# Three reorderings of DMA issues in a fused gated-recurrence and maxout kernel: the first gate tile in two halves, two weight pieces ahead of unit 3's k and q, and a late placing of w1 times w_out

## The chip, the cores and the metric

The kernel runs on one core of one Trainium2 chip. The metric is device time in microseconds, from the first to the last instruction and what lies around it; lower is better. A core has five engines that run their own instruction streams and wait for each other by semaphores: TensorE (PE in the profile, with PEld for its weight loads), VectorE (DVE), ScalarE (ACT), GpSimd (POOL) and SyncE (SP). SP computes nothing; here it issues nearly all DMAs, and an instruction that only issues a DMA stands in the profile under SPq or ACTq.

## The reference

```python
q, k, v, f_logit: (4, 8, 768, 48) float32          # batch, heads, time, head dimension
f = 1 / (1 + exp(-f_logit))
for t in range(768):
    state = f[:, :, t, :, None] * state + einsum('bhd,bhe->bhde', k[:, :, t], v[:, :, t])
    y[:, :, t] = einsum('bhd,bhde->bhe', q[:, :, t], state)
x = y.transpose(0, 2, 1, 3).reshape(3072, 384)
out = maximum(maximum(x @ w1, x @ w2), x @ w3) @ w_out   # w1, w2, w3: 384 x 768; w_out: 768 x 384
```

The weights w1, w2, w3 and w_out arrive as 64-bit floats and are rounded to float32 on the chip.

## The kernel before, in words

**Units.** The recurrence is cut in chunks of 64 time steps. A unit is one chunk of two batches, so there are 24 units (NU), and four of them (GRP) make a group of 512 tokens that goes through the feed-forward part together. For each unit the program calls, among others:

- `load(u)`, which loads f, k and q, and `load_v(u)`. Units 0 to 5 (u < BY_ROWS) are loaded by rows of time, one DMA of 192 KB for each of f, k and q (line 174). From unit 6 on, one call with an even u loads f, k or q of two units in eight smaller DMAs (line 183). v takes two DMAs per unit (line 164).
- `sigmoids(u)`: the gate. For the first six units PE transposes f (L291) and ACT takes the sigmoid of it (L308); later ACT works on the loaded blocks (L311).
- `scan(u)`: for later units DVE turns the gate (L296, tile `gate`), then runs a scan (L329, tile `r`).
- `after(u)` and `before(u)`: the decayed keys kh (L340) and queries qh (L351). For later units DVE turns k and q (L296, tiles `kt` and `qt`), there is a second scan between them (L347, tile `prod`), and POOL does the multiplications.
- `keys_by_blocks`: DVE turns kh back (L382, tile `ks`). `pairs`, `values`, `sums`, `finish`: the matmuls of the recurrence. `pack`: two DMAs that fill gaps in `xT`, the transposed x of a group (L524).

**Weights.** There are 24 pieces of 384 KB. `load_weights(count)` issues the next `count` of them on SP (L218); the first three go to tiles `raw`, the next nine to `placed`. A piece is then rounded by ACT (L240, L241, L244), DVE (for the first three pieces L251 and L252) and POOL (L258), and w1's piece is subtracted from those of w2 and w3 (L752).

**The feed-forward part.** `ffn_first` handles group 0 while it rounds the weights, with plain matmuls (L542). It also computes w1 times w_out (`linear`, L783) into `w_nat`, which is a part of the tile `w_in[0]`. Its function `place(dst, src, n)` copies 48-row strips of a weight within on-chip memory to the head-by-head layout of later groups, in ten DMAs for one weight (L458, L465). `placed[1]` receives w3 less w1; `w_lin`, another part of `w_in[0]`, receives `w_nat`. `ffn(g)` handles groups 1 to 5 (PE L881 for the inputs, L629 for the outputs) with fewer products, for which POOL and DVE form sums (`hm`, L899, L924, L931, L932, L593). For group 1 alone, the function `fourth(0)` calls `mix_x`, POOL's first reader of `w_lin` (L585); PE reads `w_lin` after that.

**Order.** The whole program stands in a manual schedule: each engine runs its instructions in the order in which the Python code emits them. The feed-forward part is cut into steps by Python generators; `fill(ns)` emits steps until an estimated budget of TensorE time is used, and so mixes them with the units. SP's order is also the order of the code. The main loop runs over u from 4 to 23; what it emits at u belongs mostly to unit u + 1. In it, `load(u + 2, one, "q")` at u = 8 loads q of units 10 and 11. Each new DMA takes one of eight semaphores in turn and first waits for the DMA that used it eight DMAs earlier.

**The start.** The order of the first issues is written out by hand, on SP but for three of them on ACT:

```python
load(0, both)                      # f, q on SP; k on ACT
load(1, (nc.scalar, nc.sync))      # f, q on ACT; k on SP
load_v(0)
load(2, one, "f")
load_v(1)
load(2, one, "kq")
load(3)
load_weights(3)
load_v(2)
load_v(3)
load_weights(6)
```

Of the kernel before, what the change touches and what calls it, by code (L numbers as in the profile page):

```python
# [9 lines left out]
FP32 = mybir.dt.float32  # L10
# [36 lines left out]
C = 64  # L47
# [8 lines left out]
def kernel(  # L56
# [13 lines left out]
    B, H, S, D = q.shape  # L70
# [4 lines left out]
    NK = DM // 128  # L75
    DFF = moe_w1.shape[1]
    NJ = DFF // 128
    GRP = 4
# [6 lines left out]
    w_in = [const.tile([128, NK, DFF], FP32, name=f"w_in{i}") for i in range(3)]  # L85
    w_out = const.tile([128, NJ, DM], FP32, name="w_out")
    w_nat, w_lin = w_in[0][:, :, 0:DM], w_in[0][:, :, DM:2 * DM]
    low = const.tile([1, 1], I32, name="low")

    def fast():  # L90
        ctx = ExitStack()
        with ctx:
# [48 lines left out]
            NAMES = "fkq"  # L141
# [25 lines left out]
            def load(u, queues=one, names="fkq"):  # L167
                for nm, src in (("f", f_logit), ("k", k), ("q", q)):
                    if nm not in names:
                        continue  # L170
                    if u < BY_ROWS:

                        c, bp = divmod(u, 2)
                        queues[NAMES.index(nm) % 2].dma_start(  # L174
                            out=rows[nm][u % 4][:, :, 0:D],
                            in_=src[2 * bp:2 * bp + 2, :, c * C:(c + 1) * C, :].rearrange("b h t d -> t b h d"))
                    elif u % 2 == 0:
                        t0 = u // 2 * C
                        for n in range(C // 32):
                            for par in range(2):  # L180
                                for e0, w in ((0, 32), (32, D - 32)):
                                    p0 = par * DP + e0
                                    nc.sync.dma_start(
                                        out=blocks[nm][u // 2 % 2][p0:p0 + 32, n, :, 0:w],
                                        in_=src[:, par::2, t0 + n * 32:t0 + (n + 1) * 32, e0:e0 + w].rearrange(
                                            "b h t d -> t (b h) d"))

            def load_v(u, queues=one):
                load_tokens(v_tiles[u % NLD], v, u, queues)
# [603 lines left out]
            def ffn_first(xT):  # L793
                hm = new_hm()
                steps = [(j, slice(n * HALF, (n + 1) * HALF)) for n in range(2) for j in range(J_HALF)]
                steps += [(j, slice(0, TOK)) for j in range(J_HALF, NJ)]
                n_step = 0
                for j, t in steps:
                    w = t.stop - t.start
                    for i in (1, 2):  # L800
                        p = yield from product(xT, j, i, t)
                        if i == 1:
                            nc.scalar.copy(hm[:, j, t], p)
                        else:
                            nc.vector.scalar_tensor_tensor(hm[:, j, t], hm[:, j, t], 0.0, p, op0=ALU.max, op1=ALU.max)
                        round_to(ROUNDED[n_step])
                        load_weights(2, rounded[0] - 1)
                        yield (1 if w == TOK else NK) * w * COLUMN
                        n_step += 1
                        if n_step in TURNED:  # L810
                            yield from turn(TURNED[n_step])
                for n in range(2 * NK + 2):
                    place(placed[0].bitcast(FP32), w_in[1], n)
                for a in range(NK):
                    for n, cost in enumerate(linear(a)):
                        round_to(rounded[0] + 1)
                        if a == 0 and n:
                            mix(n - 1)
                        if a == 0 and n == NK - 1:
                            mix(n)  # L820
                        yield cost
                for dst, src in ((placed[1].bitcast(FP32), w_in[2]), (w_lin, w_nat)):
                    for n in range(2 * NK + 2):
                        place(dst, src, n)
                mix(3)
                made = [[lambda jj=jj: sums_of_hm(hm, jj, slice(0, 2))] for jj in range(HJ)]
                made[-1] += [lambda jj=jj: sums_of_hm(hm, jj, slice(2, 3)) for jj in range(HJ)]
                made += [[], [], [], [], [], []]
                made += [[lambda jj=jj: sums_of_hm(hm, jj, slice(3, 4)) for jj in range(HJ)]]
                made += [[lambda: mix(4)]] + [[lambda n=n: mix_in(n)] for n in range(2)]  # L830
                made = iter(made)
                for cost in outputs_by_pairs(0, hm, xT):
                    for make in next(made, ()):
                        make()
                    yield cost
# [162 lines left out]
            with tc.manual_schedule():  # L998
# [3 lines left out]
                load(2, one, "f")  # L1002
                load_v(1)
                load(2, one, "kq")
                load(3)
                load_weights(3)
                load_v(2)
                load_v(3)
                load_weights(6)
                xT = x_tiles[0]  # L1010
                sigmoids(0)
                scan(0)
# [64 lines left out]
                for u in range(GRP, NU):  # L1077
                    n = u + 1
                    part = EARLY if u < BY_ROWS else LATER if u < 2 * GRP else PART
                    if n == BY_ROWS:  # L1080
                        scan(n)
                    fill(part)
                    keys_by_blocks(u, 2)
                    room_of_unit = room_of_pairs()
                    if u > GRP:
                        values(u - 1)
                        sums(u - 1, room_of_unit)
                    keys(u)
                    pairs(u, room_of_unit)
                    if u > GRP:  # L1090
                        finish(u - 1, xT)
                        if u % GRP == 3:
                            pack(0, 2, xT)
                        elif u % GRP == 0:
                            pack(3, 3, xT)
                    if u % GRP == 0:
                        if u > GRP:
                            packed[u // GRP - 1] = xT
                            pending.append(ffn(u // GRP - 1, xT))
                        xT = x_tiles[u // GRP % 2]  # L1100

                    if u + 2 <= BY_ROWS:
                        load(u + 2)
                    if u == BY_ROWS:
                        load(u + 2, one, "f")
                    elif u + 1 != BY_ROWS and BY_ROWS <= u + 3 < NU and u % 2:
                        load(u + 3, one, "fkq" if u % GRP == 1 else "f")
                    if u + 2 < NU:
                        load_v(u + 2)
                    keys_by_blocks(u, 3)  # L1110
                    if n < NU:
                        if n < BY_ROWS or n == BY_ROWS + 2:
                            sigmoids(n)
                        if n != BY_ROWS:
                            scan(n)
                    fill(part)
                    if n < NU:
                        after(n)
                        before(n)
                    if u == 2 * GRP:  # L1120
                        mix_in(2, nc.vector)
                    check_range(u - CHECKS, 0)
                    fill(part)
                    if BY_ROWS < u + 2 < NU and u % GRP == 0:
                        load(u + 2, one, "k")
                    if u == BY_ROWS:
                        load(u + 2, one, "kq")
                    if n < NU:
                        carry(n)
                    else:  # L1130
                        values(u)
                    check_range(u - CHECKS, 1)
                    fill(part)
                    if BY_ROWS < u + 2 < NU and u % GRP == 0:
                        load(u + 2, one, "q")
                    if n == NU:
                        finish(u, xT)
                        pack(3, 3, xT, both)
                        packed[u // GRP] = xT
                    keys_by_blocks(n, 0)  # L1140
                    fill(part - 1000 if u < 2 * GRP else part)
                    keys_by_blocks(n, 1)
                    check_range(u - CHECKS, 2)
                    if u + 2 >= CHECKS:
                        check_load(u + 2 - CHECKS)
                    if BY_ROWS <= u + 2 < NU and u != BY_ROWS:
                        sigmoids(u + 2)
# [269 lines left out]
```

## Time and profile before

| | |
|---|---|
| time of three runs | 408.34 us median, 408.01 to 408.77 |
| profiled execution, its own time | 408.11 us |
| span of the profiled execution | 406.4 us (the other 1.7 us lie around it) |
| PE busy | 390.6 us, 96% |
| DVE busy | 298.4 us, 73% |
| POOL busy | 256.4 us, 63% |
| ACT busy | 181.1 us, 45% |
| DMA: HBM read, written | 37.75 MB, 4.72 MB; mean 104 GB/s |
| granted TensorE clock | 1.000 |

The share of busy time is a mean over very different stages. By 40 slices of about 10 us, PE is below nine tenths only in the first four; DVE is at nine tenths in many slices up to about 325 us and then falls off. Over the first 60 us the DMA engines are busy most of the time.

### The profile page before, as it was taken

What the parts mean: (1) busy time and instruction counts of PE and PEld (TensorE: products, weight loads), DVE (VectorE), ACT (ScalarE), POOL (GpSimd) and SP (SyncE); (2) the same over time, 40 slices, a digit from 0 to 9 for tenths busy, and PEclk for the clock granted to TensorE, in tenths of its full rate; (3) what the DMA queues carried; (4) which work ended last, traced back from release to release, by engine and by line L of the source; (5) the groups of instructions that cost most, each with busy time, mean ns of one, the idle gap of its engine ahead of it and who ended that gap; (6) DMA issues with size and microseconds to landing.
All of it is one profiled execution on the core that took longest, in us unless ns stands there. A gap on an engine that the chain in (4) does not pass through costs nothing.

```text
span 406.4 us, 11673 instructions
## 1 busy us (share of the span) xinstructions
PE 390.6 (96%) x4658; PEld 339.5 (84%) x4658; DVE 298.4 (73%) x572; ACT 181.1 (45%) x431; POOL 256.4 (63%) x283
## 2 busy tenths in 40 slices
PE   4988999999999999999999999999999999999994
PEld 4766765559998888998889988899988899988994
DVE  6997797999988999897998997998995450012500
ACT  2479787422224441435442344523354335576210
POOL 2179695779997797397586277667477850525710
PEclk9999999999999999999999999999999999999999
DMA  8988996767367576476645376634573003541002
GB/s 173 241 260 251 275 244 88 156 93 147 92 96 115 74 156 134 84 120 85 125 109 99 57 116 88 150 83 81 77 158 86 1 19 102 131 152 47 2 19 63
DMA packets 181594, 47.21 MB, mean 116 GB/s; under 512 B 160480, under 2 KB 179232, under 8 KB 181536
## 3 DMA queue, kind: packets, MB, share of 16 engines
q1 hardware_dynamic: 178048, 45.62, 54.7%
q10 hardware_dynamic: 3488, 0.81, 1.0%
q8 instruction: 37, 0.61, 0.7%
q14 instruction: 21, 0.17, 0.1%
HBM read 37.75 MB, written 4.72 MB: 104 GB/s over the span
## 4 chain that ended last, share of the span: by engine, by line
PE 83%; DVE 6%; SPq 3%; POOL 3%; DMA 2%; issue 1%; ACT 1%; POOLq 0%
PE p L629 18%; PE p L881 17%; PE tr L881 15%; PE tr L629 13%; PE p L542 7%; PE y L415 3%; PE p L783 3%; PE a L396 2%; PE y L504 2%; PE a L433 2%; SPq L174 2%; DMA raw<-in_moe_w_dram 2%; DVE ks L382 1%; POOL w_in L258 1%; SPq L164 1%
## 5 line engine op out<-in xcount | busy, mean ns | idle before, releaser
L382 DVE STREAM_TRANSPOSE ks<-kh 32x128 f32<-32x128 f32 x256 | 77.4, 302 | 11.1 <-POOL kh L340 6.9
L881 PE MATMUL tr<-xT,placed 128*128 128x256 f32 x180 | 44.4, 384 | 0.0
L339 POOL COPY ends<-r 128x8 f32<-128x8 f32 x24 | 8.6, 357 | 48.7 <-DVE r L329 48.7
L881 PEld LDWEIGHTS tr<-xT,placed 128*128 128x128 f32 x180 | 33.6, 190 | 4.8
L329 DVE TENSOR_TENSOR_SCAN r<-gate,from_one 128x520 f32<-128x520 f32 x24 | 33.2, 1382 | 6.0 <-ACT gate L308 2.8
L340 POOL TENSOR_TENSOR kh<-kt,r 128x512 f32<-128x512 f32 x18 | 31.9, 1772 | 8.5 <-DVE kt L296 8.5
L542 PE MATMUL p<-xT,w_in 128*128 128x256 f32 (+1 forms) x108 | 33.9, 458 | 3.3 <-POOL w_in L752 2.2
L593 POOL TENSOR_TENSOR w_in<-hm 128x256 f32<-128x256 f32 x18 | 13.3, 739 | 32.2 <-DVE hm L932 29.5
L511 ACT COPY xT<-y 64x256 f32<-64x256 f32 (+1 forms) x60 | 22.1, 368 | 22.0 <-PE y L504 21.3
L347 DVE TENSOR_TENSOR_SCAN prod<-gate,from_inv 128x520 f32<-128x520 f32 x24 | 31.6, 1317 | 0.0
L881 PE MATMUL tr<-xT,w_in 128*128 128x256 f32 x120 | 30.8, 379 | 0.0
L881 PE MATMUL p<-w_in,placed 128*128 128x256 f32 x120 | 30.4, 382 | 0.0
L637 DVE TENSOR_TENSOR o<-tr,w_in 128x384 f32<-128x384 f32 (+1 forms) x11 | 5.7, 521 | 33.4 <-PE tr L629 29.0
L542 PEld LDWEIGHTS p<-xT,w_in 128*128 128x128 f32 x108 | 19.5, 190 | 12.3 <-issue 6.0
L629 PE MATMUL p<-placed,hm 128*128 128x192 f32 x144 | 29.7, 333 | 0.0
L881 PE MATMUL p<-xT,placed 128*128 128x256 f32 x120 | 29.2, 379 | 0.0
L629 PE MATMUL tr<-w_out,w_in 128*128 128x192 f32 x144 | 28.6, 326 | 0.0
L924 DVE TENSOR_TENSOR hm<-tr,hm 128x512 f32<-128x512 f32 x15 | 10.3, 684 | 22.8 <-PE tr L881 15.9
L258 POOL TENSOR_TENSOR w_in<-top_bits,rest_bits 128x384 uint32<-128x384 uint32 x18 | 21.7, 1215 | 7.6 <-DVE top_bits L252 4.7
L881 PEld LDWEIGHTS p<-w_in,placed 128*128 128x128 f32 x120 | 22.4, 190 | 4.4 <-issue 1.5
L634 ACT COPY w_in<-p 128x384 f32<-128x384 f32 x15 | 7.2, 479 | 41.8 <-PE p L629 41.8
L280 ACT ACTIVATE raw<-top_bits 128x384 f32<-128x384 f32 x48 | 25.2, 526 | 0.4
(168 smaller groups left out, 995.6 us busy)
## 6 DMA issues: line engine op xcount, KB each, us to landing
raw<-in_moe_w_dram SPq DMA_DIRECT2D x24, 384.0 KB, 4.5
v_ld<-in_v_dram SPq DMA_DIRECT2D x48, 96.0 KB, 3.4
placed<-in_moe_w_dram SPq DMA_DIRECT2D x12, 384.0 KB, 5.9
out_dram<-o SPq DMA_DIRECT2D x45, 96.0 KB, 2.2
placed<-in_moe_w_out_dram SPq DMA_DIRECT2D x6, 384.0 KB, 5.4
f_ld<-in_f_logit_dram SPq DMA_DIRECT2D x36, 64.0 KB, 2.9
k_ld<-in_k_dram SPq DMA_DIRECT2D x36, 64.0 KB, 2.5
q_ld<-in_q_dram SPq DMA_DIRECT2D x36, 64.0 KB, 2.5
```

The costliest lines, as they stand in the source:

```text
L258: nc.gpsimd.tensor_tensor(dst, by(top), by(rest), op=ALU.add)
L280: nc.scalar.activation(over, size, AF.Relu, scale=(-1 / HI_MIN, 1.0)[step - 1], bias=(1.0, -HI_END * (1 - 2.0 ** -24))[step - 1], accum_ou ...
L329: nc.vector.tensor_tensor_scan(r[:, 0:LEN][:, ::-1], flat(gate)[:, ::-1], flat(from_one)[:, ::-1], 1.0, op0=ALU.mult, op1=ALU.max)
L340: (nc.vector if u < BY_ROWS else nc.gpsimd).tensor_tensor(kh.rearrange("p h a t -> p a h t"), kt, by_batch(r[:, 1:LEN + 1].rearrange("p (x ...
L347: nc.vector.tensor_tensor_scan(flat(prod), flat(gate_tiles[u % 2]), flat(from_inv[u % 2]), 1.0, op0=ALU.mult, op1=ALU.max)
L382: nc.vector.transpose(ks[n * 32:(n + 1) * 32, :, par, e0:e0 + 32], kh[p0:p0 + 32, :, a, t0:t0 + 32])
L415: nc.tensor.matmul(y[o:o + DP, a, hp * C:(hp + 1) * C], lhsT=v_ld[s, 2 * hp + par, :], rhs=d["at"][s, par, hp, :], start=(hp == 0), stop=F ...
L511: nc.scalar.copy(xT[o, :, t0 + a * C:t0 + (a + 1) * C], y[i, a, 0:HP * C].rearrange("p (h t) -> p h t", h=HP))
L542: nc.tensor.matmul(p if w < TOK else p.rearrange("p (two t) -> p two t", two=2), lhsT=w_in[i][:, kt, j * 128:(j + 1) * 128], rhs=x[:, t.st ...
L593: engine.tensor_tensor(dst, x, y, op=op)
L629: nc.tensor.matmul(b[:, p * HD:(p + 1) * HD], lhsT=x, rhs=w, start=id(b) not in begun, stop=True, skip_group_check=True)
L881: nc.tensor.matmul(b[:, j * HALF:(j + 1) * HALF], lhsT=w[:, (2 * n + j) * 128:(2 * n + j + 1) * 128], rhs=x, start=begin and j == 0, stop= ...
```

## The change

1. f of unit 0 is loaded by two DMAs of 64 partitions (32 time steps of both batches) each. The first half goes to SP, the second to ACT, where it stands ahead of unit 0's k. One DMA is added to the program.
2. At the start, the first two weight pieces are issued between f and k of unit 3; the third stays behind unit 3's q. Unit 3's v moves behind the six pieces of `placed`.
3. The ten DMAs that place `w_nat` into `w_lin` move from the end of `ffn_first`'s weight work, right behind the placing of `placed[1]`, to the main loop at u = 8, behind q of units 10 and 11. On SP they now stand behind `pack` of group 1, f, k and q of units 10 and 11 and v of units 9 and 10.

The order of the instructions on PE, DVE and POOL is the same before and after; ACT has one DMA issue more.

```diff
@@ load @@
                         c, bp = divmod(u, 2)
-                        queues[NAMES.index(nm) % 2].dma_start(
-                            out=rows[nm][u % 4][:, :, 0:D],
-                            in_=src[2 * bp:2 * bp + 2, :, c * C:(c + 1) * C, :].rearrange("b h t d -> t b h d"))
+                        parts = 2 if u == 0 and nm == "f" else 1
+                        for i in range(parts):
+                            n = C // parts
+                            t0 = c * C + i * n
+                            queues[(NAMES.index(nm) + i) % 2].dma_start(
+                                out=rows[nm][u % 4][2 * i * n:2 * (i + 1) * n, :, 0:D],
+                                in_=src[2 * bp:2 * bp + 2, :, t0:t0 + n, :].rearrange("b h t d -> t b h d"))
@@ ffn_first @@
-                for dst, src in ((placed[1].bitcast(FP32), w_in[2]), (w_lin, w_nat)):
-                    for n in range(2 * NK + 2):
-                        place(dst, src, n)
+                for n in range(2 * NK + 2):
+                    place(placed[1].bitcast(FP32), w_in[2], n)
@@ the start @@
                 load(2, one, "kq")
-                load(3)
-                load_weights(3)
+                load(3, one, "f")
+                load_weights(2)
+                load(3, one, "kq")
+                load_weights(1)
                 load_v(2)
+                load_weights(6)
                 load_v(3)
-                load_weights(6)
@@ the main loop @@
                     if BY_ROWS < u + 2 < NU and u % GRP == 0:
                         load(u + 2, one, "q")
+                    if u == 2 * GRP:
+                        for part_of in range(2 * NK + 2):
+                            place(w_lin, w_nat, part_of)
```

## The prediction

> **What bounds the kernel now.** I read the engine totals and the 40 slices first: is one engine the bound, and where is it not?
>
> ```profile
> PE 390.6 (96%) x4658; PEld 339.5 (84%) x4658; DVE 298.4 (73%) x572; ACT 181.1 (45%) x431; POOL 256.4 (63%) x283
> ...
> PE   4988999999999999999999999999999999999994
> ```
>
> PE is the bound, and no edit touches its instructions. So the change can only move PE's 15.8 us of idle time (406.4 less 390.6). It lies in the first 40 us, which hold four slices under nine tenths, and in what the waits of PE name. In the window 0 to 160 us they list (engine, line, whom it waited for: total us, times, longest):
>
> ```profile
> PE tr L291 <- DMA f_ld<-in_f_logit_dram: 5.0, 1, 5.0
> PE p L542 <- POOL w_in L752: 2.2, 3, 1.3
> ...
> PE p L629 <- DVE hm L931: 0.6, 1, 0.6
> ```
>
> After 160 us no wait of PE is listed. So what PE has gained by 160 us stays to the end, unless a new wait arises. Next the timeline of the start (start, length, engine, line, what):
>
> ```profile
> 0.89 0.77 ACTq L174 DMA_DIRECT2D k_ld<-in_k_dram  x1
> 0.92 0.79 SPq L174 DMA_DIRECT2D f_ld<-in_f_logit_dram  x1
> ...
> 4.97 1.08 PE L291 MATMUL tr<-ident,f_ld 128*128 128x128 f32 x4 [4.97 <-DMA f_ld<-in_f_logit_dram]
> ...
> 6.09 0.60 ACT L308 ACTIVATE gate<-tr 128x512 f32<-128x512 f32 x1 [1.51 <-PE tr L291]
> ...
> 6.78 1.24 DVE L329 TENSOR_TENSOR_SCAN r<-gate,from_one 128x520 f32<-128x520 f32 x1 [2.46 <-issue]
> ```
>
> f lands, PE turns it, ACT makes the gate, DVE scans. From 6.78 DVE is busy almost without a gap (9.64 of the 10 us from 10 to 20) up to the first late weight piece, which the chain of waits shows:
>
> ```profile
> 12.80 0.88 SPq L218
> 13.69 0.04 issue
> 13.73 7.13 DMA raw<-in_moe_w_dram
> 20.86 0.02 issue
> 20.89 1.14 DVE top_bits L251
> ```
>
> The second piece takes 7.13 us from its issue and ends DVE's wait at 20.86. DVE itself had been idle for only 0.23 us, so its own work and this DMA are nearly tied. From there the chain runs over DVE and POOL (L251, L252, L258, L752) to PE, which is full from 40 us on. The last stretch comes from the timeline and the chain between 123 and 159 us:
>
> ```profile
> 123.72 4.37 SPq L183 DMA_DIRECT2D q_ld<-in_q_dram  x8
> ```
>
> ```profile
> 128.01 1.20 DVE L347 TENSOR_TENSOR_SCAN prod<-gate,from_inv 128x520 f32<-128x520 f32 x1
> 130.16 0.71 DVE L296 STREAM_TRANSPOSE qt<-q_ld 128x512 f32<-128x512 f32 x1 [0.95 <-DMA q_ld<-in_q_dram]
> ```
>
> ```profile
> 156.68 0.69 DVE hm L931
> 157.37 0.04 issue
> 157.41 0.59 PE p L629 x2
> 158.01 0.59 PE p L629 x2
> ```
>
> q of unit 10 is issued until 128.09 and DVE stands 0.95 us for it. DVE then has hardly a gap until 157, where PE waits for DVE twice, for L931 and L932.
>
> **What the Trainium skill says.** (1) "DMA: Bandwidth & Descriptors", section "Issuing engines are not separate DMA queues": DMAs from SP and ACT run on the same engines, and two issuers save only issue time. So I credit edit 1 with nothing for its second queue, only for what stands behind f. The trace shows shared service: k, issued 0.03 us ahead of f on the other queue, delays f. (2) The same page, section "Queues, rings and completion order": within one queue descriptors are consumed in ring order. So a piece moved ahead of k and q takes their place, and they take its. (3) "SBUF — State Buffer", section "Who interferes with whom": a DVE instruction with two on-chip inputs and a GpSimd instruction that reads on-chip memory exclude each other. The trace agrees: POOL's kh of unit 10 takes 2.02 us beside the 1.20 us scan, its qh 1.18 us. I need this for edit 3.
>
> **Edit 1, f in halves.** It adds one DMA on ACT. In the window from 4 to 8 us the DMAs move 258 to 259 GB/s; k's 197 kB (192 KB) there take 0.76 us. Before, they are served ahead of or among f's; after, both halves of f come first. At most the whole 0.76 is saved, at least about 0.4 if k still mixes in; I take 0.55. ACT's added issue costs about 0.65 us (0.70 for f there, 0.63 the shortest for v), so the table load 3.30 to 4.58 ends near 5.23; the gate, at 6.09 − 0.55 = 5.54, just clears it. k's transposes need k at about 5.3, and it lands where f did, under 4.97. Each later DMA waits for the one eight earlier, one place shifted; these have landed. **0.55 us** on the path.
>
> **Edit 2, weights ahead of k and q of unit 3.** The two pieces are issued 1.75 us sooner (at 11.04 in place of 12.80: k took 0.70, q 0.97, plus gaps). Their landing at 20.86 or before then moves to about 19, ahead of a DVE that arrives at 20.66 − 0.55 = 20.11. The 0.23 us of idle goes: **0.23 us**, bounds 0 and 0.4. What is late next: k and q of unit 3 now end where the second piece did, about 20.9; PE wants them at 22.43 and 22.81, less 0.8. The third piece lands at 14.27 + 7.8 = 22.1, DVE wants it at 23.17 − 0.8 = 22.4. v of unit 2 lands at 17.09 + 5.5 = 22.6, PE wants it at 23.45 − 0.8 = 22.65. All just fit: they cap the gain near 0.8. The pieces of `placed` lose 192 KB ahead of them, about 0.8 us at the 243 GB/s of this stage; ACT waited 2.3 us for them in two places (1.53 of it at 24.59), but DVE is the later partner there, so I count nothing. v of unit 3 goes behind six pieces, wanted only at 37.44: nothing, with some 4 us of cover.
>
> **Edit 3, the late placing.** Ten DMAs, 6.76 us of SP time (101.00 to 107.76), leave their place. On SP that lets `pack`, f, v, k and q of units 10 and 11 go earlier by up to that: q then lands near 123.2 instead of about 130.0. DVE loses its 0.95 at `qt` and the 0.17 listed at `kt`. But `ks`, next on DVE, waits for POOL's kh: that ended at 130.19 and moves only by the 0.17. So `ks` at 130.80 becomes about 130.08: **0.72 us**. Bounds 0 and 1.1. PE's two waits at 157 are DVE's, so PE gains the same, if DVE holds the lead for 27 us. The placing itself now ends about 128.1 on SP and lands by 131 (about 2.4 us). POOL wants `w_lin` at 138.88: 7 us of cover. SP's later issues (the check's load, f of unit 12 at 128.67) start as before, since the sum of SP's work is the same.
>
> **Sum.** 0.55 + 0.23 + 0.72 = **1.5 us** off the profiled execution's 408.11: 406.6. The median of the runs is 408.34, 0.2 above it, so the forecast is **406.8 us**. About 0.8 us (0.2%) is what a measurement can tell from no change.
>
> **Rivals.** (a) *Only the start pays*: DVE, relieved of q, waits on POOL instead at kh, qh or the sums, since POOL was at 8.45 of 10 us between 130 and 140. Then 0.8 us: 407.5. For it: the lock above. Against it: POOL had 1.6 us of idle there itself. Chance 0.17. (b) *Only the placing pays*: the third piece, v of unit 2 or the table load holds the start. Then 0.7: 407.6. For it: covers of 0.05 to 0.3 us. Chance 0.15. (c) *Nothing pays*, or f's halves are served as late as f was, and POOL absorbs edit 3: 408.3. Chance 0.1. (d) *Slower*: k and q of unit 3 stand behind 768 KB of weights. PE runs in order; behind their transposes are `values(2)` and the first product. Before, they were some 8 us early, so nothing measured covers the new place. It turns from gain to loss when q lands later than 22.8; at 24.5 it costs 1.7 us, 410.0 if edits 1 and 3 do not pay and 409.3 if edit 3 does. For it: the landings of 5.5 to 8 us in that stage, up from 3 to 4 before the weights. Chance 0.1. The main case keeps 0.48; its own range is 405.7 to 407.4.
>
> **How the numbers follow.** The range goes from 405.7 (1.5 plus the upper bounds, 0.2 + 0.2 + 0.4, near 2.3, and some for ACT's vanished waits) to 408.6, which takes in (a), (b) and (c) and leaves out most of (d). Faster by over 0.8: the main case nearly whole, 0.46, and half of (a) and (b), 0.16, makes 0.62, and 0.04 for more gain from ACT; same: the rest of (a), (b) and (c), 0.22; slower: (d), 0.12 with unforeseen lateness.
>
> **What would show it.** Right: the first PE matmul at 4.4 and DVE's first scan at 6.2; no DMA wait of DVE near 20; no DMA wait at `qt` near 129; PE without the waits for L931 and L932; POOL's first L585 not waiting for a DMA. Wrong: PE waiting for k or q of unit 3 near 22, a late first scan, or the same PE wait for `hm` near 156.

## The result and the profile after

The changed kernel takes **405.55 us** (median of five runs, 405.47 to 406.43) against 408.34 for the kernel before in the same comparison: a ratio of 0.9937, 95% interval 0.9921 to 0.9953, or 2.8 us. The forecast was 406.8, that is 1.5 us less, with a range of 405.7 to 408.6: the median lies 0.15 us below the range. The profiled execution took 405.47 us for a span of 403.7; before, it was 408.11 and 406.4. Most lines of the changed kernel have numbers three to eight higher than in the kernel before (L291 is L295, L296 is L300, L477 is L481, L504 is L508). L931 and L932 are L934 and L935 there, but a kernel with edit 1 and without edit 3 has them at L935 and L936.

First the page's totals and PE's row of the 40 slices:

```profile
PE 390.9 (97%) x4658; PEld 339.7 (84%) x4658; DVE 297.7 (74%) x572; ACT 180.9 (45%) x431; POOL 256.4 (64%) x283
...
PE   5988999999999999999999999999999999999995
```

PE does the same work in a shorter span. Its waits from 0 to 160 us (engine, line, whom it waited for: total us, times, longest):

```profile
PE tr L295 <- DVE q_ld L148: 4.4, 1, 4.4
PE p L546 <- POOL w_in L756: 1.9, 2, 1.3
...
PE p L295 <- DMA k_ld<-in_k_dram: 0.3, 1, 0.3
...
PE y L415 <- DMA v_ld<-in_v_dram: 0.2, 1, 0.2
```

The wait for L931 (0.6 us before) is gone, and no wait for it under a new number has come. The first wait is 4.4 us in place of 5.0. It is put down to a memset of DVE that happened to end near it; the second half of f landed at 4.27, and PE starts 0.13 us after that, as it started 0.14 us after f's landing at 4.83 before. Two small new waits are there, for k of unit 0 and v of unit 2. The timeline of the start:

```profile
0.89 0.76 ACTq L178 DMA_DIRECT2D f_ld<-in_f_logit_dram  x1
0.92 0.78 SPq L178 DMA_DIRECT2D f_ld<-in_f_logit_dram  x1
...
1.68 0.68 ACTq L178 DMA_DIRECT2D k_ld<-in_k_dram  x1
...
4.40 1.08 PE L295 MATMUL tr<-ident,f_ld 128*128 128x128 f32 x4 [4.40 <-DVE q_ld L148]
...
5.53 0.60 ACT L312 ACTIVATE gate<-tr 128x512 f32<-128x512 f32 x1
...
6.22 1.24 DVE L333 TENSOR_TENSOR_SCAN r<-gate,from_one 128x520 f32<-128x520 f32 x1 [1.90 <-issue]
```

First matmul and first scan are both 0.57 us earlier. The next lines are from DVE's timeline near 20 us:

```profile
20.01 0.36 DVE L255 TENSOR_SCALAR top_bits<-raw 128x384 uint32<-128x384 uint32 x1
20.40 1.25 DVE L256 SCALAR_TENSOR_TENSOR top_bits<-raw,top_bits 128x384 uint32<-128x384 uint32 x1
22.00 0.69 DVE L403 TENSOR_TENSOR at<-a,mask 128x512 f32<-128x512 f32 x1 [0.34 <-PE a L400]
```

No bracket names a DMA: the second piece, which ended DVE's wait at 20.86 before, landed at 16.71. From L371 at 26.30 (27.25 before) PE is 0.95 us ahead. The chain of waits there runs no longer over a weight piece but over v of unit 2, issued at 17.77:

```profile
17.77 5.66 DMA v_ld<-in_v_dram
23.42 0.04 issue
23.47 1.13 PE y L415 x28
```

Then the stretch of edit 3, from the timeline:

```profile
116.01 4.15 SPq L187 DMA_DIRECT2D q_ld<-in_q_dram  x8
...
126.43 0.71 DVE L300 STREAM_TRANSPOSE kt<-k_ld 128x512 f32<-128x512 f32 x1 [0.17 <-DMA w_in<-w_in]
...
128.19 0.68 DVE L300 STREAM_TRANSPOSE qt<-q_ld 128x512 f32<-128x512 f32 x1
...
129.28 1.24 DVE L386 STREAM_TRANSPOSE ks<-kh 32x128 f32<-32x128 f32 x4 [0.42 <-POOL kh L344]
```

q of unit 10 is issued by 120.16 in place of 128.09. DVE no longer waits at `qt`, but for POOL's kh at `ks`, for 0.42 us. The idle 0.17 us at `kt` is still there. Last, the chain at 156 us:

```profile
155.86 0.42 PE p L633 x2
156.28 0.01 issue
156.29 0.59 PE p L633 x2
```

The matmul that stood behind the wait at 157.41 starts at 155.69, and PE keeps these 1.71 us to its last instruction (399.56 against 401.27 at its end).

### The profile page after: what moved, and what is told of

It reads as the page before. It is cut to its first block, busy times and chain, and to the rows that moved or that the text cites. A ratio compares the mean times of both kernels' runs of the same rounds, so it can differ in the third digit from the quotient of the medians.

```text
span 403.7 us, 11683 instructions
## 1 busy us (share of the span) xinstructions
PE 390.9 (97%) x4658; PEld 339.7 (84%) x4658; DVE 297.7 (74%) x572; ACT 180.9 (45%) x431; POOL 256.4 (64%) x283
## 4 chain that ended last, share of the span: by engine, by line
PE 90%; SPq 4%; DMA 1%; ACT 1%; issue 1%; POOL 1%; DVE 0%
PE p L884 20%; PE p L633 18%; PE tr L884 16%; PE tr L633 14%; PE p L546 7%; PE y L419 3%; PE p L787 3%; PE a L400 2%; PE y L508 2%; PE a L437 2%; SPq L178 2%; DMA v_ld<-in_v_dram 1%; SPq L164 1%; SPq L222 1%; PE tr L295 1%
## 5 line engine op out<-in xcount | busy, mean ns | idle before, releaser
L927 DVE TENSOR_TENSOR hm<-tr,hm 128x512 f32<-128x512 f32 x15 | 10.3, 684 | 22.8 <-PE tr L884 15.9
```

## The experiments

Two theories stood at the outset: A, that start and placing are terms which add up, with edits 1 and 2 in series in the start (f sets the first scan, the second weight piece sets DVE at 20.9 us), and a set of rivals, in which some term is lost. The first four runs led to a third, G: **SP's queue is a clock of its own** between about 80 and 130 us. Each experiment was timed beside runs of the kernel before on the same chip, on three chips in all. There the kernel before stood at 409.8 to 410.1 us (medians of 40 to 70 runs), not at 408.3, and scattered from 406.6 to 413.6. So ratios are compared, and for mechanisms the traces. A shift is always against the first profile of before.

### Edit 1 alone, edit 2 alone

On the kernel before, in one kernel the new lines of `load`, in the other those of the start:

```diff
-queues[NAMES.index(nm) % 2].dma_start(
+parts = 2 if u == 0 and nm == "f" else 1
+for i in range(parts):
...
+    queues[(NAMES.index(nm) + i) % 2].dma_start(
```

```diff
-load(3)
-load_weights(3)
+load(3, one, "f")
+load_weights(2)
+load(3, one, "kq")
+load_weights(1)
 load_v(2)
-load_v(3)
 load_weights(6)
+load_v(3)
```

> Edit 1 alone on the kernel before. Theory A (the two start edits are in series: f sets the first scan, the second weight piece sets DVE at 20.9 us): the first PE matmul moves from 4.97 to about 4.4 and the first scan from 6.78 to 6.2, but the second weight piece still lands near 20.9, so DVE and PE are at their old times from there on: PE's last instruction, at 401.27 before, moves by 0 to 0.2 us, and the time stays within 0.3 us of 408.3. Rival B (as my prediction's sum had it, each start edit pays for itself): PE's last instruction moves by 0.55 us and the time is about 407.7. Rival C (a part of the 2.8 us comes from edit 1 in the tail): over 1 us gained.

> Edit 2 alone on the kernel before. Theory A: the second weight piece is no longer late, DVE loses its wait of about 0.2 to 0.4 us near 20 us, the first scan stays at 6.78: PE moves by 0.2 to 0.4 us from 27 us on, the time is about 408.0. Rival B (prediction): 0.23, not told apart from A by this run alone. Rival D (k and q of unit 3 become late): PE waits for a DMA near 22 us and the time is 408.5 or more.

Measured: ratios 0.9983 (0.9962 to 1.0005) and 0.9971 (0.9953 to 0.9989). Both did in the start what they should. With the halves the first matmul came at 4.40 and PE's first product (24.88 before) 0.90 us earlier: here the second piece landed at 19.60, so theory A's "in series" was wrong. With the weights alone PE was 0.30 us ahead at 24.58. But in neither profile did the lead reach 160 us. By the times something was left on the average: 0.3% with the weights, clear of noise, and 0.2% with the halves, which is not. Of the halves alone, the timeline and PE's waits:

```profile
125.35 4.32 SPq L187 DMA_DIRECT2D q_ld<-in_q_dram  x8
...
132.72 0.71 DVE L300 STREAM_TRANSPOSE qt<-q_ld 128x512 f32<-128x512 f32 x1 [3.27 <-DMA q_ld<-in_q_dram]
```

```profile
PE y L508 <- ACT seen L426: 1.5, 1, 1.5
PE a L400 <- POOL qh L355: 0.8, 1, 0.8
...
PE p L633 <- DVE hm L935: 0.7, 1, 0.7
```

DVE waits 3.27 us for q of unit 10, which landed at 132.44. PE stands for it later, at 134.7 (for POOL's qh, which is made from `qt`), 152.1 and 160.0. Where the kernel before has 134 us, PE was still 0.34 us ahead, and where it has 157, PE was 2.55 us behind. With the weights alone the same wait was 2.11 us, and PE 0.87 us behind.

### Edit 3 alone, edits 1 and 2 together

Edit 3 alone on the kernel before is this; the other kernel has both diffs above and not this one.

```diff
-for dst, src in ((placed[1].bitcast(FP32), w_in[2]), (w_lin, w_nat)):
-    for n in range(2 * NK + 2):
-        place(dst, src, n)
+for n in range(2 * NK + 2):
+    place(placed[1].bitcast(FP32), w_in[2], n)
...
 if BY_ROWS < u + 2 < NU and u % GRP == 0:
     load(u + 2, one, "q")
+if u == 2 * GRP:
+    for part_of in range(2 * NK + 2):
+        place(w_lin, w_nat, part_of)
```

> Edit 3 alone on the kernel before. Theory A: q of unit 10 lands some 6 us earlier, DVE loses its wait of 0.95 us at qt and PE its wait of 0.6 us for L931: PE moves by 0.7 to 0.8 us at 157 and keeps it, the time is about 407.5. Rival E (POOL takes the wait over, or the gain needs the earlier start): PE's last instruction moves by less than 0.2 us, 408.2.

> Edits 1 and 2 together, the placing where it was before. Theory A: PE moves by 0.95 us at 26 us as in the changed kernel. SP's placing follows PE's work, so the lead survives q of unit 10: PE's last instruction moves by 0.95 us, the time is about 407.3. Rival F (SP's queue is full and keeps its own time, so q of unit 10 lands where it did and eats the lead): PE's wait for hm near 156 grows to 1.2 to 1.6 us, PE's last instruction moves by less than 0.2 us, 408.2. Against both: if the 2.8 us come whole from the order of the start, this run shows 405.6.

Measured: edit 3 alone 0.9928 (0.9907 to 0.9949), as much as the whole change brought on another chip (below); edits 1 and 2 together 0.9994 (0.9967 to 1.0020), nothing that can be measured. The expectation for edit 3 was too small, and theory A's for the start fell. Of edit 3 alone:

```profile
129.80 0.68 DVE L296 STREAM_TRANSPOSE qt<-q_ld 128x512 f32<-128x512 f32 x1
```

There is no bracket: q had landed at 126.52, 3.3 us ahead. PE was 0.66 us behind at 150 us, from a loss at 41 us (below), and 0.11 us ahead at 157.41. This gain of 0.77 to 0.78 us between 150 and 157 us is in all eight profiles with edit 3. In the pair of start edits `qt` began at 133.13, 2.97 us later than before, as q landed at 132.85. But this run had lost its lead already at 42 us (below), so it does not show by itself that q ate it; the two runs above do.

### What PE follows at 157 us, and the kernel before again

The six profiles with the placing ahead of q (the first profile of before, the second below, the three above and one more below) have `qt` at 130.16, 131.79, 132.72, 131.02, 133.13 and 131.30. PE's matmul behind the wait (157.41 before) starts 27.24 to 27.26 us after it in all six. Whether PE was ahead at 40 us does not enter. So rival F holds in its main part: what was gained before is lost at q. In the eight profiles with edit 3 as it is in the changed kernel the distance is 27.49 to 27.51 us, from a `qt` that waits for no DMA but only for what DVE does before it; PE does not wait there.

SP has no gap over 0.5 us between its issues from 80 to 130 us, in any of the 14 profiles. Single issue instructions stretch from 0.49 to between 1 and 2 us, at other places in each run. Thus q comes when SP's sum is done.

> The kernel before once more, for a second profile of it. Theory G: SP issues back to back from about 95 to 150 us, the stretches of its issue instructions differ from run to run, and q of unit 10 lands where SP's sum puts it: between 130 and 134 us. DVE's wait for it at qt is 1 to 3.5 us, and PE waits at L504 or for hm L931 for what is over about 0.7 us of it. If instead q lands at 130.0 as in the first profile while the time is near 410, the lateness of q does not explain the larger gain on such chips.

The kernel before, profiled once more (409.99 us for this execution), is as expected:

```profile
131.79 0.71 DVE L296 STREAM_TRANSPOSE qt<-q_ld 128x512 f32<-128x512 f32 x1 [2.19 <-DMA q_ld<-in_q_dram]
```

PE was 1.63 us later at 157 than in the first profile, exactly as `qt`. The first profile, from which I sized edit 3, had the earliest q of the six: it landed at 129.98, the others at 130.84 to 132.85.

> The changed kernel, but with the ten DMAs that place w1 times w_out ahead of q of unit 10 in place of behind it; f, v and k of units 9 and 10 stay early. Theory G: only q's time on SP counts, so q lands at about 130 again, DVE waits at qt for it, PE waits near 150 or 157, and the gain shrinks to between 0 and 0.7 us against before, with the scatter of before. Rival H (k, f or v of the moved group carries the gain): like the changed kernel.

On the changed kernel:

```diff
+if u == 2 * GRP:
+    for part_of in range(2 * NK + 2):
+        place(w_lin, w_nat, part_of)
 if BY_ROWS < u + 2 < NU and u % GRP == 0:
     load(u + 2, one, "q")
-if u == 2 * GRP:
-    for part_of in range(2 * NK + 2):
-        place(w_lin, w_nat, part_of)
```

Measured: 0.9992 (0.9970 to 1.0015). Moving the placing ahead of q alone takes the whole gain away:

```profile
124.81 4.36 SPq L187 DMA_DIRECT2D q_ld<-in_q_dram  x8
...
131.30 0.71 DVE L300 STREAM_TRANSPOSE qt<-q_ld 128x512 f32<-128x512 f32 x1 [2.46 <-DMA q_ld<-in_q_dram]
```

f, v and k of the group were issued 1.4 to 2.1 us later than in the first profile of the changed kernel (f from 102.70), but 4.7 to 6.5 us earlier than before. So rival H is out, and G's reading of edit 3 is shown: it is q's place on SP.

### The changed kernel again, and with one start edit each

The first is the changed kernel itself; the other two are edit 3 with one of the first two diffs above.

> The changed kernel once more, beside runs of before on the same chip. Theory G, formed after the first four runs: between about 95 and 150 us SP issues back to back, so q of unit 10 comes at SP's own time. Without edit 3, whatever PE has gained before waits there for q (PE waits near 150 and 157 us); edit 3 takes 6.3 us out of SP's way, so the start's lead passes through, and DMA scatter of 1 to 3 us is absorbed too. Expected: no DMA wait of DVE at qt, no wait of PE at L508 or for hm L935, and on a chip where before stands at about 410 a gain over before of 3 to 4 us (ratio 0.990 to 0.993). Theory A (three terms that add): 2.0 us below before wherever it runs, and no nearer to it in scatter.

> Edits 2 and 3 without the halves of f. Theory G: first scan at 6.78, the lead of edit 2 alone (0.3 us at 24 to 27 us, as in its run alone) and no loss near 150: 0.3 us below edit 3 alone by PE's last instruction, that is about 0.6 us later than the changed kernel. Theory A says the same size; the difference is in the waits near 150.

> Edits 1 and 3 with the weights where they were. Theory G: first PE matmul 4.4, a lead of 0.55 to 0.95 us at 24 to 36 us (0.95 in the run of edit 1 alone), kept through 150 us; the time is within 0.4 us of the changed kernel's, so that edit 2 is worth little beside edit 1. If edits 1 and 2 are in series (the second piece sets DVE at 20.9 us): no lead at 27 us and the time of edit 3 alone.

Measured: 0.9928 (0.9900 to 0.9955); without the halves 0.9926 (0.9898 to 0.9954); without the weights 0.9937 (0.9913 to 0.9961). The changed kernel scattered by 2.3 us here (11 runs, 405.79 to 408.11), the kernel before by 5.0 (40 runs). Its timeline:

```profile
119.00 5.36 SPq L187 DMA_DIRECT2D q_ld<-in_q_dram  x8
...
128.14 0.68 DVE L300 STREAM_TRANSPOSE qt<-q_ld 128x512 f32<-128x512 f32 x1
```

SP was 4 us later with q than in the first profile (issued until 124.36, landed 126.61), and no engine waited for it: that is the cover which edit 3 adds. PE's last instruction ended at 399.50, against 399.56 in the first profile. It ended at 400.12 without the halves, 0.6 us later as expected, and at 401.45 without the weights, later than expected (the first matmul at 4.52, a lead of 0.33 us at 27 us, and then a loss). PE's waits and timeline of that last kernel:

```profile
PE p L481 <- ACT w_in L780: 1.1, 1, 1.1
```

```profile
42.07 0.19 PE L481 MATMUL p<-st 128*1 128x1 f32 x2 [1.11 <-ACT w_in L780]
```

The wait for ACT is in truth one for a DMA: ACT rounds the first of the three pieces of `placed` that are issued near 33 us as soon as it has landed. In the seven profiles in which PE waits here, its L481 (L477) starts 3.51 to 3.54 us after that landing. In the changed kernel the piece landed at 36.18 and 36.34, early enough; before at 37.22, which lets only 0.37 us of a lead pass (41.12 less 37.22 less 3.53). With edit 2 DMAs work through the stretch from 20 to 24 us (by windows of 2 us, DMA share 0.86 and 1.09 in the changed kernel, 0.45 and 0.70 before), and the piece comes about 1 us earlier. That the one brings the other was not tested, and it is no guarantee: of nine profiles with the order of edit 2 or a like one, five have the piece at 35.85 to 36.75, but four at 37.2 to 38.6 (edits 1 and 2 together among them, where PE waited 1.5 us); of the five without it, none before 37.16.

### The start: order or split, and how far k and q can go back

> The changed kernel with f of unit 0 whole again, and f, k and q of units 0 and 1 all on SP, so that nothing stands ahead of or beside f. Only the start is read; SP's later issues come about 2 us later and cost time further on. If the order is what counts (k no longer ahead of f): first PE matmul at 4.4 or before, as with the halves. If the two queues count (rival): about 4.7 to 5.0.

> The changed kernel with both halves of f of unit 0 on SP, and k first on ACT as before. If the order counts: k is served first again and the second half is issued 0.8 us later, first PE matmul at 5.0 or later. If the mere split counts (smaller transfers): under 4.7.

> The changed kernel with all three first weight pieces and v of unit 2 ahead of k and q of unit 3. It tries my rival (d). k and q landed at 18.1 and 18.8 in the changed kernel, PE wants them at 21.9 and 22.4. They move behind 384 KB and 192 KB more, 576 KB at 242 GB/s or 2.4 us: 20.5 and 21.2. Theory: still in time, no wait for k or q, v of unit 2 lands about 22 in place of 23.4 and PE's wait of 0.2 us for it goes; PE's last instruction within 0.2 us of the changed kernel's. Rival (d): PE waits 0.5 us or more for k or q near 22 us and does not recover.

Three changes to the changed kernel, one each, in the order of the expectations:

```diff
-parts = 2 if u == 0 and nm == "f" else 1
+parts = 1
...
-load(0, both)
-load(1, (nc.scalar, nc.sync))
+load(0, one)
+load(1, one)
```

```diff
-queues[(NAMES.index(nm) + i) % 2].dma_start(
+queues[NAMES.index(nm) % 2].dma_start(
```

```diff
-load_weights(2)
-load(3, one, "kq")
-load_weights(1)
+load_weights(3)
 load_v(2)
+load(3, one, "kq")
```

The timelines' first matmul of PE, f whole and first, and then both halves with k first:

```profile
4.24 1.09 PE L295 MATMUL tr<-ident,f_ld 128*128 128x128 f32 x4 [4.24 <-DMA f_ld<-in_f_logit_dram]
```

```profile
6.21 1.09 PE L295 MATMUL tr<-ident,f_ld 128*128 128x128 f32 x4 [6.21 <-DMA f_ld<-in_f_logit_dram]
```

**The order counts, not the split or the second queue.** Whole and alone in front, f landed at 4.11; in halves behind k it landed at 4.51 and 6.08, the second half beside f of unit 1, which ACT had issued meanwhile. The times (0.9982, 0.9953 to 1.0010, and 0.9958, 0.9940 to 0.9976) say little of the start: in the first kernel SP's later issues come later too, and PE waited 1.4 us at 41 us. The second kernel's profile shows that beside edit 3 the start goes through to the end: PE runs 0.87 us behind the kernel before from 27 to 150 us, gains its 0.77 at 157, and ends at 401.39, 1.8 us after the changed kernel.

With k and q of unit 3 behind three pieces and v of unit 2, PE's timeline near 22 us:

```profile
21.85 0.66 PE L295 MATMUL tr<-ident,k_ld 128*128 128x128 f32 x4
22.46 0.63 PE L295 MATMUL tr<-ident,q_ld 128*128 128x128 f32 x4
23.02 1.17 PE L415 MATMUL y<-v_ld,at 64*64 64x48 f32 x32
```

k and q landed at 21.30 and 22.33 (20.5 and 21.2 expected) and PE still waits for neither; its wait for v is gone. So rival (d) needs over 3 us more than what the change did to them: its turning point (22.8 us before, less the lead; PE takes q at 22.46) is still not passed here. PE's L371 was at 26.30 as in the changed kernel. The second part of the expectation failed: PE ended at 402.63, as the piece of `placed` landed at 38.13 and PE waited 1.4 us at 41 us. The ratio is 0.9926 (0.9902 to 0.9950), not told apart from the changed kernel. No kernel is shown to be faster than the changed one. Edit 3 covers q alone: this kernel and the one with f whole, whose piece came late in their profiles, scattered by 5.5 and 6.3 us.

## Why the prediction was right, and where it was not

All that it named as signs of being right is in the first profile: the first matmul at 4.40, the first scan at 6.22, no DMA wait of DVE near 20 us or at `qt`, no wait of PE for L931 or L932, and no DMA wait of POOL at the first use of `w_lin`.

- **Edit 1, 0.55 us.** Measured 0.57 at the first matmul and at the first scan. The reason given (k no longer ahead of f) is shown by the two orders. What the Trainium skill says under "DMA: Bandwidth & Descriptors", section "Issuing engines are not separate DMA queues", held: one queue with f alone in front was 0.16 us better than two with halves. The table load ended at 5.45, 0.08 us ahead of the gate (5.23 expected). One side effect was missed: k landed at 5.66, not under 4.97, and PE waited 0.31 us for it, off the path.
- **Edit 2, 0.23 us, bounds 0 and 0.4.** Together with edit 1 the lead at 26 us is 0.95 us, so 0.38 for edit 2 in this pair of profiles; alone it gave 0.30. But the halves alone gave 0.95 with their second piece at 19.60, so the division between the two depends on when the piece lands, which differed by over 1 us between runs. The trade agrees with what the Trainium skill's "DMA: Bandwidth & Descriptors", section "Queues, rings and completion order", states, that each DMA engine consumes descriptors in ring order: the pieces landed at 15.61 and 16.71 in place of 18.93 and 20.86, k and q at 18.13 and 18.83 in place of 14.67 and 16.23. Of the named limits, one was seen: v of unit 2 landed at 23.42 (22.6 expected) and cost 0.2 us, which PE had made up by 26 us.
- **"The pieces of `placed`: I count nothing."** This step was wrong. They are a second gate, at 41 us: without an earlier piece only 0.37 us of the lead could pass.
- **Edit 3, 0.72 us.** In the pair of profiles 1.71 less 0.95 is 0.76, and `ks` waits for POOL's kh with 0.42 us, as the step said: kh again takes 2.02 us beside the scan. But the number is right in part by luck. The 0.17 us at `kt` were taken for a wait for q; they stay, beside whatever DMA is under way, so kh does not move beyond the lead and `ks` gains 0.57 (130.80 to 129.28, less 0.95). The other 0.2 came on DVE later: its L932 behind took 1.30 us before and 1.02 after. Why is open.
- **The sum.** Where 1.5 us were predicted, PE gains 1.71 in the profiles; with all three edits the terms do add up, because q is early by far. What was wrong is that each term had a worth of its own. q was taken to be 0.95 us late for DVE; but if DVE comes 0.95 us earlier and SP does not, it is twice as late, and without edit 3 the start is worth between nothing and 0.3%, by the three ratios. The right form is a maximum of DVE's order and SP's clock. And SP's clock scatters: `qt` came up to 2.97 us later than in the profile that I used. Where before stands at 410, edit 3 is worth 0.7% of the time by itself.
- **Rivals.** (b), only the placing pays, came nearest in the times of the later chips, but not for its reason: without edit 3 the start's lead is not held up at the start, it is lost at q. What the start adds beside edit 3 is not resolved by the times there (intervals of about 1 us to each side); it shows in the end of PE's work alone, 399.50 for the changed kernel against 401.16 with edit 3 alone, 0.66 us of it lost at 41 us. (a) and (c) fell: POOL did not absorb edit 3, and its L589 at 137.13, the first reader of `w_lin`, waits for no DMA. (d) did not come near; of its "some 8 us early" before, 7.8 were right for k, but q had 6.6.
- **From 1.71 to 2.8 us.** Of the 2.64 us between the two profiled executions, 0.93 lies behind PE's last instruction: 6.84 us from there to the execution's own end before, 5.91 after. The prediction looked for PE's idle time in the first 40 us and in PE's waits, but 5.1 of the 15.8 us stand behind PE's last instruction. Nothing ties this part to the change. Over all 14 profiles this tail is 5.86 to 5.92 in five and 6.5 to 7.1 in nine, with the changed kernel once in each group (5.91 and 6.88), at PE ends of 399.56 and 399.50. The last DMA of the output landed 2.57 to 2.68 us after PE's last instruction in the five and 3.28 to 3.81 us after it in the nine. What makes it late, and how it was spread over the timed runs of the first comparison, is open.

## What to carry to other kernels

Gains at different places of a program do not add when a queue between them keeps its own time: ask of each early gain which transfers it will meet sooner, and whether these move with it. When an issuing engine runs without a gap, an issue that is needed late belongs behind those needed early, and the worth of that is the scatter it covers as well as the wait in one profile. Ahead of the first dependent work, put the transfer it waits for first; splitting it over two queues was only a way to do so.

## What the hardware showed that I had not expected

- After PE's wait of 1.4 to 1.5 us at 41 us the granted clock fell to one half for 3.4 us. By windows of 1 us of edits 1 and 2 together (window, length, busy us and count of PE, PEld, DVE, ACT and POOL, granted clock, DMA share, GB/s):

```profile
41.00:42.00 1.00, 0.14 (x5) 0.10 (x5) 0.00 (x0) 1.00 (x4) 0.96 (x2) 1.00 1.09 378
...
44.00:45.00 1.00, 1.00 (x6) 1.00 (x6) 1.00 (x1) 0.86 (x2) 0.00 (x0) 0.50 1.09 376
45.00:46.00 1.00, 1.00 (x4) 0.82 (x3) 0.93 (x3) 0.97 (x3) 0.19 (x1) 0.50 1.10 410
```

  PE's lag grew by 1.4 us in it, as much as the wait itself. All three profiles with a wait of 1.4 us or more here show it, those with 1.1 us or less do not; but a wait of 1.5 us near 152 us (halves alone) did not bring it on, and in the second profile of before the clock was at one half from 29.45 to 32.86 with no single wait above 0.8 us ahead of it. So the length of one wait does not decide. The traces show a nearer measure. Each of the four drops lasts 3.41 us and begins six or ten times 3.41 us after the first clock record of its trace (8.97 and 29.45 in the second profile of before, 9.24 and 43.38 with edits 1 and 2). The stretch of 3.41 us that ends at the drop, for the second before, edits 1 and 2, k and q behind three pieces, and f whole; then, on the same grid, edits 1 and 3 (wait of 1.1 us) and the halves alone, both without a drop:

```profile
26.04:29.45 3.41, 1.94 (x40) 1.24 (x39) 3.27 (x6) 3.20 (x8) 3.33 (x3) 1.00 0.97 312
39.96:43.37 3.41, 1.95 (x42) 1.22 (x41) 0.65 (x2) 2.65 (x8) 2.00 (x2) 1.00 1.09 370
40.10:43.51 3.41, 1.98 (x42) 1.37 (x41) 0.29 (x1) 2.65 (x7) 1.64 (x2) 1.00 1.08 376
40.90:44.32 3.42, 2.02 (x42) 1.46 (x43) 0.12 (x2) 2.69 (x7) 1.35 (x2) 1.00 1.08 379
40.25:43.66 3.41, 2.29 (x44) 1.54 (x43) 0.90 (x2) 2.65 (x7) 2.17 (x3) 1.00 1.08 370
150.70:154.11 3.41, 1.98 (x38) 1.76 (x39) 3.28 (x9) 1.82 (x6) 3.33 (x5) 1.00 0.91 235
```

  PE was busy for 57 to 59% of a stretch that ended in a drop. Of the stretches on this grid that begin before 397 us, in all 14 profiles, every other one had at least 62%, but for the last line, whose 58% brought none; why is open. The Trainium skill, "TensorE: Matmul & The Clock Gate", section "HAM oscillation — how this bites in real kernels", asks for no PE idle gap above about 3.4 us; here single waits of less than half of that were enough, with the other idle time around them, so the measurement decides.
- An instruction that only issues a DMA is no constant: eight equal ones took 4.15 us in the changed kernel's first profile and 5.36 in its second. On a queue without gaps this adds up: the first of these eight began at 116.01 in the one and at 119.00 in the other.
